# Casting one product's operand for the second pair earlier, and opening the first mixer's PSUM pools in the output stage

## The chip, the cores and the metric

The kernel runs on one NeuronCore of one Trainium2 chip. The metric is device time in microseconds (us); every kernel is run several times, and the median counts. All timelines are in microseconds from the start of the profiled span.

## The reference

The input is a sequence of 2048 rows of 1024 values. First comes a linear-attention block with 32 heads, then an MLP that mixes over the sequence (token mixer), each behind a layer norm and with a residual.

```python
def _A_ref(x, wqkv, wo):                       # linear attention, H = 32 heads of 32
    q, k, v = split_heads(x @ wqkv)
    phi = lambda t: where(t > 0, t + 1, exp(t)) + 1e-6
    pq, pk = phi(q), phi(k)
    kv, z = einsum("bhsd,bhse->bhde", pk, v), einsum("bhsd->bhd", pk)
    o = (pq @ kv) / (pq @ z + 1e-6)
    return merge_heads(o) @ wo

def _B_ref(x, w1, b1, w2, b2):                 # token mixer
    h = layernorm(x)
    u = gelu(einsum("bsd,sf->bdf", h, w1) + b1)     # 2048 -> 3584 over the sequence
    y = einsum("bdf,fs->bds", u, w2) + b2           # 3584 -> 2048
    return y.transpose(0, 2, 1)

h = x + _A_ref(layernorm(x), wqkv, wo)
out = h + _B_ref(layernorm(h), w1, b1, w2, b2)
```

## The kernel before

The program has four stages, one after the other on TensorE (PE): the projections for keys, values and queries; the output projection of the attention (the output stage), which also makes the residual `h`, its layer-norm statistics and the normalised rows `hE` (even row tiles) and `hO` (odd ones); the first mixer (w1 and gelu, giving `gE` and `gO`); and the second mixer (w2, written out). Around the change the order on each engine is the order in which the program is written, since nearly all instructions there are pinned (`Held`, `pin`).

**The mixer's scheme.** A mixer's matrix product is done as a two-by-two block product with seven products instead of eight (Strassen's scheme in Winograd's form). `Product7` holds the seven: `p1`, `p5`, `p6`, `p2`, `p7`, `p3`, `p4`. Each has a stationary operand `lhs[m]` made of weight blocks a11, a12, a21, a22, and a moving operand `mov[m]` made of `hE`, `hO` and the sums `hT2`, `hT3`, `hT4`. The results pass through PSUM tiles `psA`, `psB`, `psC`, `psE`: `p1` computes psA and ScalarE (ACT) copies it to psB; `p6` adds into psB and ACT copies that to psC; `p2`, `p7`, `p3` and `p4` add the rest, and each quarter ends in a gelu on ACT.

**Pairs and their pairs.** A `Quad` is a pair of `Mixer1` column blocks that share one set of weights (u = 0 to 6). Some of a pair's products are themselves done by seven smaller products (`Inner`: steps `i1`, `i6`, `i2`, `i5`, `i7`, `i3`, `i4`, with psI tiles of 256 columns). `interleave` puts the smaller products between pieces of the large ones, and calls functions at named points ("b", "c", "2", "7", "third", "end"). `run_first` does the pair u = 0, `run1` the pair u = 1, `run1_six` the rest.

**Product 7's operand.** It is a21 - a11, a tile named `sa` (tag `sa7`, one buffer). For u = 0 VectorE (DVE) makes it in the output stage. From u = 1 on `cast7(q)`, for the quarters q = 0 to 3, writes -a11 with an ACT instruction; after quarters 1 and 3 `add_a21` issues a DMA from POOL (line 164) that adds half of a21 from DRAM, 256 KB. `run1` calls the four at the points "c", "2", "7" and "third" of its first interleaved product. The matmuls of product 7 (`p7_fill`) use the eight blocks of the operand in the order 2, 3, 4, ... 7, 0, 1 (`first = NSP // 4`), so the third matmul already needs the second DMA. `cast5` does the same for product 5, with a22 as the cast half and the weight tile itself (`wq`) as the destination.

**The turn from the output stage to the first mixer.** The output stage works through 16 row tiles; it ends, for the last of them, with the ACT evacuations of two PSUM tiles `acc_t`, BN_STATS and BN_AGGR on DVE, `h_scale` (two small ACT instructions: Ln into `hln_l`, Exp into `sc_all`), `normalize_h` and the sums `sums_h` on DVE. Then the output stage's PSUM pools are closed, the mixer's pools `psz`, `psw`, `psx`, `psy` are opened, and `run_first` starts with `p1` of both column blocks, each with its copy from psA to psB behind it.

Helpers issue most of this, so nearly all of its instructions carry line 247, and the tile names tell them apart.

Of the kernel before, what the change touches and what calls it, by code (L numbers as in the profile page):

```python
# [16 lines left out]
PSUM = bass.MemoryType.PSUM  # L17
# [18 lines left out]
def kernel(  # L36
# [44 lines left out]
    def less_acc():  # L81
        accx.close()
        acc_ring[:] = [acc]
# [136 lines left out]
    hmov = {}  # L220
# [321 lines left out]
    class Quad:  # L542
# [251 lines left out]

        def run_first(self, nxt, before_inner, before_second):
            sts = self.sts
            for st in sts:
                st.p1()
            share(sts)
            for st in sts:  # L800
                st.p2()
            before_inner(slice(0, 2))
            self.in5.mov = self.mov5
            self.interleave(self.in5, self.steps(*[st.p6 for st in sts]), {
                "2": lambda: nxt.cast5(0), "7": lambda: nxt.cast5(1), "third": lambda: nxt.cast5(2), "end": lambda: nxt.cast5(3),
            })
            before_inner(slice(2, 4))
            nxt.begin1()
            self.base3()
            for i, st in enumerate(sts):  # L810
                st.apart = 1
                st.p7()
                before_second(slice(2 * i, 2 * i + 2))
            sts[0].p3()
            sts[1].p3_mm()
            self.late.append(sts[1].p3_evac)
            return sts, nxt
# [105 lines left out]
        def run1(self, pend, nxt, on_p4, third_sums, sums6):  # L923
            sts = self.sts
            s4, s6, s7 = self.steps(*[st.p4 for st in pend]), self.steps(*[st.p6 for st in sts]), self.steps(*[st.p7_fill for st in sts])
            c6, c7 = 3 * len(s6) // 4, len(s7) // 2

            def starting():
                self.in1.sums(slice(2, 4))
                self.in5 = Inner(sts, 5, self.mov5, next(Quad.tags), self.sink5, self.sum5)  # L930
                self.in5.sums(slice(0, 2))
                self.asums(6)
                self.t1 = self.base("t1a")
                for s, st in enumerate(sts):
                    st.begin(self.t1[:, s, :])

            def gelu(s, dh, t):
                return lambda: sts[s].evac(0, dh, t[:, s, :])

            def before_gelu():  # L940
                if third_sums is not None:
                    third_sums(slice(3, 4))
                gelu(0, 0, self.t1)()

            def gelu_late(*args):
                return lambda: self.late.insert(0, gelu(*args))

            self.in1.behind = self.late
            self.interleave(
                self.in1, s4, {  # L950
                    "b": starting, "c": lambda: self.cast7(0), "2": lambda: self.cast7(1),
                    "7": lambda: (self.in5.sums(slice(2, 4)), self.cast7(2)), "third": lambda: self.cast7(3),
                }, (("b", None), ("7", None))
            )
            in2 = Inner2(sts, 2, self.mov2, next(Quad.tags), self.add_to(self.t1), None)
            in2.sums()
            on_p4()
            nxt = nxt()
            share(sts)
            if third_sums is not None:  # L960
                third_sums(slice(0, 3))
            self.interleave(self.in5, s6[:c6], {
                "b": lambda: (sums6(slice(0, 1)), self.asums(3)), "third": lambda: (nxt.cast5(0), nxt.cast5(1)),
            }, flush=(("b", None), ("7", None), ("end", None)), first=1)
            sts[0].finish()
            self.base3()
            in3 = Inner2(sts, 3, self.mov3, next(Quad.tags), self.add_to(self.t3), None)
            in3.sums()
            sts[0].with_shared(sts[0].base3, sts[0].B)
            self.interleave(  # L970
                in2, s6[c6:] + s7[:c7], {
                    "2": lambda: (nxt.cast5(2), sums6(slice(1, 2))), "7": lambda: nxt.cast5(3), "third": lambda: (before_gelu(), sums6(slice(2, 4))), "end": gelu_late(1, 0, self.t1),
                }, (("7", None),)
            )
            sts[1].with_shared(sts[1].base3, sts[1].B)
            self.interleave(in3, s7[c7:], {
                "third": lambda: (gelu(0, 1, self.t3)(), nxt.begin1()), "end": gelu_late(1, 1, self.t3),
            }, (("b", 1), ("c", None)))
            return sts, nxt
# [13 lines left out]
    with ExitStack() as actx:  # L993
# [757 lines left out]
        with ExitStack() as a3:  # L1751
# [121 lines left out]
            def h_scale(i):  # L1873
                lnv = a3s.tile([P, 1], F32, name="hln_l")
                share_of = 1.0 / D if i in BY_ACT else 1.0
                hs.activation(lnv[:], mv_all[:, i, 1:2], ACT.Ln, bias=eps2[:], scale=(1.0 + LN_EPS) * share_of)
                hs.activation(sc_all[:, i:i + 1], lnv[:], ACT.Exp, scale=-0.5)
# [8 lines left out]
            def sums_h(us, which):  # L1886
                assert all(normal.issuperset(range(NSC * SPREAD.index(u), NSC * SPREAD.index(u) + NSC)) for u in us)
                ks = slice(NSC // 2 * us[0], NSC // 2 * (us[-1] + 1))
                e, o = hE[:, ks], hO[:, ks]
                for t in which:  # L1890
                    out, p, q = {
                        "t3": (hT3[:, ks], e[:, :, hi], o[:, :, hi]),
                        "t1": (e[:, :, hi], e[:, :, hi], e[:, :, lo]),
                        "t2": (hT2[:, ks], o[:, :, hi], e[:, :, hi]),
                        "t4": (hT4[:, ks], o[:, :, lo], hT2[:, ks]),
                    }[t]
                    hv.tensor_tensor(out, p, q, ALU.subtract)
# [52 lines left out]
            for i in range(1, NS):  # L1950
                if i > 1:
                    out_mm(i)
                if i in den_at:
                    den(den_at[i])
                if i in w1_at:
                    load_w1(*w1_at[i], pin, 4)
                if i >= SEEDED - 5:
                    load_xr(i + 5)
                if i == NS - 1:
                    h_scale(i - 1)  # L1960
                    normalize_h(i - 2)
                    normalize_h(i - 1)
                if 1 < i <= SEEDED:
                    h_mean(i - 1)
                if i - 3 in BY_ACT:
                    normalize_h(i - 3)
                if SEEDED - 2 <= i < NS - 2:
                    seed(i + 2)
                if i > 1:
                    out_evac(i)  # L1970
                if i - 3 in BY_DVE:
                    h_scale(i - 3)
                if i - 2 in BY_ACT:
                    h_var(i - 2)
                    h_scale(i - 2)
                if SEEDED < i < NS - 1:
                    h_scale(i - 1)
                if i in scale_at:
                    scale_q(*scale_at[i])
                for at in spread_at.get(i, ()):  # L1980
                    den_spread(*at)
                if i in sums_at:
                    cur = next(ahead)
                if i - 3 in BY_DVE:
                    normalize_h(i - 3)
                if i - 2 in BY_DVE:
                    h_var(i - 2)
                if SEEDED + 2 <= i < NS - 1:
                    normalize_h(i - 2)
                for at in sums_h_at.get(i, ()):  # L1990
                    sums_h(*at)
            h_scale(NS - 1)
            sums_h((1,), ("t1",))
            normalize_h(NS - 1)
            sums_h((0,), ("t1",))
            sums_h((0, 1), ("t2",))
            less_acc()

    earlyctx.close()
    actx_psum.close()  # L2000
    NT = 2
    psz = ctx.enter_context(tc.tile_pool(name="psz", bufs=NT, space=PSUM, reuse_waits="tile"))
    psw = ctx.enter_context(tc.tile_pool(name="psw", bufs=NT, space=PSUM, reuse_waits="tile"))
    psx = ctx.enter_context(tc.tile_pool(name="psx", bufs=NT, space=PSUM, reuse_waits="tile"))
    psy = ctx.enter_context(tc.tile_pool(name="psy", bufs=NT, space=PSUM, reuse_waits="tile"))
    gpool = ctx.enter_context(tc.tile_pool(name="gpool", bufs=1))
    gE = gpool.tile([P, NFP, D], FP16, name="gE")
    gO = gpool.tile([P, NFP, D], FP16, name="gO")
# [2 lines left out]
    assert NFP % 2 == 0 and NSP % 2 == 0 and NSP >= 4 and NFP >= 6  # L2011
    inner1 = mctx.enter_context(tc.tile_pool(name="inner1", bufs=1, side="right"))
    pools["i1"] = inner1
    hmov.update(moving(hE, hO, hT2, hT3, hT4))
    mov1, sums1 = inner_moving(hE[:, :, 0:CW], NSP, inner1, "hi1")
    mov5, sums5 = inner_moving(hE[:, :, CW:D], NSP, inner1, "hi5")
    mov2, sums2 = inner_moving(hO[:, :, 0:CW], NSP, inner1, "hi2")
# [13 lines left out]
    def quad1(u):  # L2031
        return Quad([Mixer1(2 * u), Mixer1(2 * u + 1)], mov1, mov5, mov2, mov3)

    Held.on = Held.scalar = True
    sums5()
    late = slice(0, NSP // 2)
    dve.tensor_tensor(hT3[:, late], hE[:, late, 0:CW], hT2[:, late], ALU.subtract)
# [198 lines left out]
```

## Time and profile before

| | |
|---|---|
| median of 3 runs | 551.63 us (550.24, 551.94, 551.63) |
| the profiled execution | 551.81 us |
| its span, first to last instruction | 550.0 us |
| mean granted TensorE clock | 0.997 |
| PE busy | 542.6 us, 99% of the span |
| DVE busy | 465.6 us, 85% |
| ACT busy | 312.5 us, 57% |
| POOL busy | 72.8 us, 13% |
| DMA | 77.76 MB, mean 141 GB/s |

A timeline row gives the start, the time from there to the end, the engine, the line, the operation, the tiles written and read, the shape and the count; in brackets stands how long the engine was idle just before and what ended that. Neighbouring instructions of one kind are merged into a row. "PEld" is PE's load of a stationary operand, which overlaps its matmuls. Instructions of one engine overlap a little in these rows, so the distance between two starts is what one really takes of the queue. The granted clock is a share of full speed.

### The profile page before, as it was taken

Reading aid. Unit: us, or ns where it says so; the run is one execution under the profiler, and the core shown is the slowest. Engines: PE = TensorE matmul, PEld = TensorE weight load, DVE = VectorE, ACT = ScalarE, POOL = GpSimd, SP = SyncE. Lnnn points to the kernel's source line nnn. Section 1 sums busy time; section 2 is a strip of 40 time slices with the busy share of each in tenths; the row PEclk is TensorE's granted clock in tenths of the full one; section 3 lists DMA queues with packets and bytes.
Section 4 is the critical chain, followed back from the end, with each engine's and each line's share of the span. In section 5 each row is a group of like instructions: output and inputs, shape, how many; then the busy total and the mean of one; then the engine's idle time right before and its main releaser. Section 6 shows DMA issues by size and latency. Waiting matters only on the chain.

```text
span 550.0 us, 10552 instructions
## 1 busy us (share of the span) xinstructions
PE 542.6 (99%) x4038; PEld 338.5 (62%) x4038; DVE 465.6 (85%) x926; ACT 312.5 (57%) x666; POOL 72.8 (13%) x78
## 2 busy tenths in 40 slices
PE   8999999999999999999899999999999999999997
PEld 3444446656864444456577777777455667877865
DVE  7798897867777578989689989999998899979877
ACT  5748677767787788657477677775320312412321
POOL 1000000000002440012012121130002103103111
PEclk9999999999999999999899999999999999999999
DMA  8933532201469999137345857656597659399344
GB/s 302 311 78 76 79 77 41 40 1 40 115 173 185 225 274 309 62 40 150 43 86 108 165 66 154 127 85 154 146 308 196 182 141 241 74 290 234 77 127 75
DMA packets 105378, 77.76 MB, mean 141 GB/s; under 512 B 16482, under 2 KB 97904, under 8 KB 105328
## 3 DMA queue, kind: packets, MB, share of 16 engines
q1 hardware_dynamic: 85536, 64.32, 42.0%
q0 software_dynamic: 19360, 12.34, 17.2%
q8 instruction: 31, 0.51, 0.4%
q10 hardware_dynamic: 432, 0.44, 0.2%
q14 instruction: 19, 0.16, 0.1%
HBM read 62.27 MB, written 11.67 MB: 134 GB/s over the span
## 4 chain that ended last, share of the span: by engine, by line
PE 84%; issue 5%; DMA 5%; DVE 3%; POOL 2%; ACT 1%; SPq 1%; POOLq 0%; ACTq 0%
PE psI L247 30%; PE psC L247 17%; PE psC L1195 4%; PE psB L1195 4%; PE psA L1195 4%; PE psB L247 4%; PE psA L247 3%; PE acc_t L1111 3%; PE acc_t L247 2%; PE psE L1195 2%; PE psA L1329 2%; PE psC L1329 2%; PE psB L1329 2%; DMA sa<-in_B_w_dram 2%; POOL h_bf L1843 2%
## 5 line engine op out<-in xcount | busy, mean ns | idle before, releaser
L247 PEld LDWEIGHTS <-is 128*128 128x128 f16 x900 | 88.5, 98 | 33.0 <-issue 0.8
L247 PEld LDWEIGHTS <-wq 128*128 128x128 bf16 (+1 forms) x694 | 67.9, 98 | 37.2 <-issue 0.7
L247 PEld LDWEIGHTS <-sa 128*128 128x128 f16 x467 | 45.7, 98 | 16.8 <-DMA sa<-in_B_w_dram 2.9
L247 PE MATMUL acc_t<-wo_sb,pqT 128*128 128x512 f16 x256 | 55.9, 379 | 0.0
L247 PEld LDWEIGHTS <-pqT 128*128 128x128 bf16 x256 | 24.8, 98 | 30.6 <-issue 1.1
L520 POOL DMA_DIRECT2D out_dram<-wq x28 | 24.3, 937 | 143.6 <-ACT wq L523 120.4
L247 PE MATMUL psC<-gs,wq 128*128 128x512 f16 x168 | 40.8, 379 | 0.0
L1843 POOL DMA_DIRECT2D h_bf<-in_A_x_dram x18 | 15.8, 984 | 185.6 <-DMA wq<-in_B_w_dram 169.7
L247 PE MATMUL psI<-hi,is 128*128 128x256 f16 x240 | 36.4, 275 | 0.0
L247 PE MATMUL psC<-hT,sa 128*128 128x512 f16 x112 | 32.9, 386 | 2.4 <-DMA sa<-in_B_w_dram 2.4
L247 PE MATMUL psC<-hT,wq 128*128 128x512 f16 x112 | 34.1, 379 | 0.0
L1195 PEld LDWEIGHTS <-xs 128*128 128x128 f16 x208 | 20.0, 98 | 22.2
L247 ACT COPY psI<-psI 128x256 f32<-128x256 f32 x60 | 21.5, 358 | 15.9 <-PE psI L247 13.8
L247 PE MATMUL psI<-gi,is 128*128 128x256 f16 x210 | 27.8, 273 | 0.0
L1195 PE MATMUL psA<-wkv,xnT 128*128 128x512 bf16 x104 | 26.7, 379 | 0.0
L164 POOL DMA_DIRECT2D wq<-in_B_w_dram x12 | 15.4, 1284 | 82.6 <-ACT wq L247 43.4
L1195 PEld LDWEIGHTS <-xnT 128*128 128x128 bf16 x156 | 15.3, 98 | 17.9 <-issue 0.2
L247 DVE TENSOR_TENSOR t<-psI,t 128x256 f32<-128x256 f32 (+1 forms) x45 | 20.2, 472 | 6.3 <-PE psI L247 5.0
L201 DVE TENSOR_SCALAR e_sb<-e_sb 128x512 bf16<-128x512 bf16 x64 | 18.1, 284 | 6.5 <-ACT e_sb L196 6.4
L164 POOL DMA_DIRECT2D sa<-in_B_w_dram x12 | 15.4, 1285 | 53.6 <-ACT sa L247 33.3
L1111 PE MATMUL acc_t<-wkv,xnT 128*128 128x512 bf16 x96 | 22.0, 379 | 0.1
L247 DVE TENSOR_TENSOR is<-wq 128x512 f16<-128x512 bf16 (+3 forms) x48 | 21.9, 457 | 0.0
(276 smaller groups left out, 1213.1 us busy)
## 6 DMA issues: line engine op xcount, KB each, us to landing
wq<-in_B_w_dram SPq DMA_DIRECT2D x20, 448.0 KB, 5.8
gs<-parked SPq DMA_DIRECT2D x9, 896.0 KB, 4.8
wq<-in_B_w_dram SPq DMA_DIRECT2D x11, 512.0 KB, 5.1
wq<-in_B_w_dram SPq DMA_DIRECT2D x5, 1024.0 KB, 7.2
shared_sb<-rd_dram SPq DMA_DIRECT2D x32, 128.0 KB, 5.1
out_dram<-h_bf SPq DMA_DIRECT2D x16, 256.0 KB, 5.1
x_sb<-in_A_x_dram SPq DMA_DIRECT2D x14, 256.0 KB, 3.9
w2o<-in_B_w_dram SPq DMA_DIRECT2D x4, 896.0 KB, 9.8
```

What stands on the lines that cost most here:

```text
L164: pin(nc.gpsimd.dma_start(t[:, ks, :], a21[:, ks, :], accum_op=ALU.add))
L201: pin(nc.vector.tensor_scalar(e_sb[:], e_sb[:], 1.0, PHI_EPS, ALU.min, ALU.add))
L247: return (lambda *a, **kw: pin(op(*a, **kw))) if self.always or getattr(Held, self.key) else op
L520: nc.gpsimd.dma_start(to, ot[:, a:b], accum_op=ALU.add)
L1111: mm = nc.tensor.matmul(pp[:, 0:CW], lhsT=xnT[:, kt, i * P:(i + 1) * P], rhs=wkv[:, kt, c * CW:(c + 1) * CW], start=(kt == 0), stop=(kt == ...
L1195: pin(nc.tensor.matmul(ps[:], lhsT=lhs[:, k, :], rhs=rhs[:, k, :], start=(start and k == 0), stop=(k == hk2 - 1), skip_group_check=True,))
L1329: pin(nc.tensor.matmul(out[:, j], lhsT=rhs[:, k, 2 * self.half + j, :], rhs=lhs[:, k], start=(start and j == 0 and k == 0), stop=(k == hk2 ...
L1843: pin(nc.gpsimd.dma_start(h_bfs[i][:, cols], x[rows(i), cols], accum_op=ALU.add))
```

## The change

Two things are done. First, `run_first` calls the four `cast7` of the next pair (u = 1) right after its two `p7`; `run1` leaves them out where the pair has the operand already. Second, the closing of the output stage's PSUM pools and the opening of the mixer's four pools move ahead of the last row tile's `h_scale`, and `p1` of the first column block (its matmuls and the copy from psA to psB) is issued there; `run_first` then issues only the second block's `p1`. On PE, DVE, POOL and SP the order of the instructions stays; on ACT the first psA copy now stands ahead of the last `hln_l` and `sc_all`, and the four casts stand behind the two `gO` gelus of product 7, ahead of the two `gE` gelus of product 3.

```diff
         def run_first(self, nxt, before_inner, before_second):
             sts = self.sts
-            for st in sts:
-                st.p1()
+            sts[1].p1()
             share(sts)
...
                 st.apart = 1
                 st.p7()
                 before_second(slice(2 * i, 2 * i + 2))
+            for q in range(4):
+                nxt.cast7(q)
             sts[0].p3()
             sts[1].p3_mm()
...
+            def cast(q):
+                return nop if 7 in self.S else partial(self.cast7, q)
+
             self.in1.behind = self.late
             self.interleave(
                 self.in1, s4, {
-                    "b": starting, "c": lambda: self.cast7(0), "2": lambda: self.cast7(1),
-                    "7": lambda: (self.in5.sums(slice(2, 4)), self.cast7(2)), "third": lambda: self.cast7(3),
+                    "b": starting, "c": cast(0), "2": cast(1), "7": lambda: (self.in5.sums(slice(2, 4)), cast(2)()), "third": cast(3),
                 }, (("b", None), ("7", None))
             )
...
+            less_acc()
+            a3p.close()
+            actx_psum.close()
+            NT = 2
+            psz = ctx.enter_context(tc.tile_pool(name="psz", bufs=NT, space=PSUM, reuse_waits="tile"))
+            psw = ctx.enter_context(tc.tile_pool(name="psw", bufs=NT, space=PSUM, reuse_waits="tile"))
+            psx = ctx.enter_context(tc.tile_pool(name="psx", bufs=NT, space=PSUM, reuse_waits="tile"))
+            psy = ctx.enter_context(tc.tile_pool(name="psy", bufs=NT, space=PSUM, reuse_waits="tile"))
+            Held.on = Held.scalar = True
+            hmov.update(moving(hE, hO, hT2, hT3, hT4))
+            cur.sts[0].p1()
             h_scale(NS - 1)
             sums_h((1,), ("t1",))
             normalize_h(NS - 1)
             sums_h((0,), ("t1",))
             sums_h((0, 1), ("t2",))
-            less_acc()
 
     earlyctx.close()
-    actx_psum.close()
-    NT = 2
-    psz = ctx.enter_context(tc.tile_pool(name="psz", ...))
-    psw, psx, psy likewise
...
-    hmov.update(moving(hE, hO, hT2, hT3, hT4))
...
-    Held.on = Held.scalar = True
     sums5()
```

More of the change, by code (lines that the diff above doesn't have):

```diff
@@ L1996 @@
             sums_h((0, 1), ("t2",))
-            less_acc()
     earlyctx.close()
-    actx_psum.close()
-    NT = 2
[L2002 to L2005, printed above, removed]
     gpool = ctx.enter_context(tc.tile_pool(name="gpool", bufs=1))
```

## The prediction

> **What bounds the kernel now.** I read the waits of TensorE (PE) first, since PE is busy nearly all the span: its table of waits has only three rows, each `us in total, times, longest`.
>
> ```profile
> PE psC L247 <- DMA sa<-in_B_w_dram: 2.4, 1, 2.4
> PE acc_t L104 <- DVE m L112: 1.2, 1, 1.2
> PE psA L247 <- ACT psB L247: 0.2, 1, 0.2
> ```
>
> The second is the program's start and is not touched. The first is one wait for product 7's operand (tile `sa`), the third one wait for the first copy psA to psB; these are exactly the two places of the change. So the time is PE's own work plus these gaps, and a change that leaves PE's work alone can win only there. The chain of waits shows what fed the first gap (start, duration, what):
>
> ```profile
> 250.49 1.28 POOL sa L164
> 251.77 1.79 issue
> 253.58 9.59 DMA sa<-in_B_w_dram
> ```
>
> The reader is to see that the second accumulating DMA was issued at 253.58 and landed only at 263.17. The timeline of PE at that place, and the windows view of the same stretch (length, busy time of PE, PEld, DVE, ACT, POOL, then the granted clock, DMA share and GB/s):
>
> ```profile
> 258.50 1.03 PE L247 MATMUL psB<-hT,sa 128*128 128x512 f16 x4
> 259.36 0.60 PE L247 MATMUL psI<-hi,is 128*128 128x256 f16 x4
> 259.80 0.60 PE L247 MATMUL psI<-hO,wq 128*128 128x256 f16 x4
> 260.24 0.59 PE L247 MATMUL psC<-hT,sa 128*128 128x512 f16 x2
> 263.21 0.61 PE L247 MATMUL psC<-hT,sa 128*128 128x512 f16 x1 [2.37 <-DMA sa<-in_B_w_dram]
> 263.61 1.06 PE L247 MATMUL psI<-hO,is 128*128 128x256 f16 x4
> 264.46 1.06 PE L247 MATMUL psI<-hi,is 128*128 128x256 f16 x4
> 265.31 1.06 PE L247 MATMUL psC<-hT,sa 128*128 128x512 f16 x2
> 266.17 0.79 PE L247 MATMUL psI<-hO,is 128*128 128x256 f16 x4
> 266.80 0.81 PE L247 MATMUL psC<-hT,sa 128*128 128x512 f16 x3
> ```
> ```profile
> 260.24:263.21 2.97, 0.60 (x5) 0.10 (x2) 1.25 (x3) 1.73 (x4) 0.94 (x1) 0.99 1.24 163
> 263.21:264.40 1.19, 1.19 (x5) 0.73 (x6) 0.00 (x0) 0.00 (x0) 0.34 (x1) 0.50 0.17 25
> 264.40:266.80 2.40, 2.40 (x13) 1.41 (x11) 1.12 (x2) 0.00 (x0) 0.00 (x0) 0.55 0.88 112
> 266.80:272.00 5.20, 5.20 (x40) 3.71 (x38) 4.86 (x10) 2.80 (x5) 0.00 (x0) 1.00 0.01 1
> ```
>
> The gap costs more than the 2.4 us that the table of waits says: after it the granted clock is 0.50, then 0.55, and back at 1.00 from 266.80.
>
> **The price of the gap.** At full clock four 512-wide matmuls take 259.36 - 258.50 = 0.86 us (0.215 each) and four 256-wide ones 259.80 - 259.36 = 0.44. From 260.24 to 266.80 PE issues five wide ones (2, 1, 2) and three groups of four narrow ones: 5 x 0.215 + 3 x 0.44 = 2.40 us of work in 6.56 us. So 4.16 us are lost: 2.54 of them idle (the third wide matmul was due at 260.24 + 2 x 0.215 = 260.67 and came at 263.21), and 1.62 at the lower clock.
>
> **Part one: the four casts of product 7 move ahead.** Nothing is added or removed: four ScalarE (ACT) instructions and two POOL DMAs for the second pair (u=1) are issued earlier, and the four later call points in `run1` become empty for this pair alone. PE, VectorE (DVE), SP and POOL keep their orders. Only ACT's changes: the casts now stand right behind the second `gO` and ahead of the `gE` of product 3. The rows of ACT there, before:
>
> ```profile
> 243.58 0.72 ACT L247 ACTIVATE gO<-t,b_sb 128x512 f16<-128x512 f32 x1 [1.20 <-DVE t L247]
> 245.56 0.72 ACT L247 ACTIVATE gE<-e,b_sb 128x512 f16<-128x512 f32 x1 [1.26 <-DVE e L247]
> 246.54 0.36 ACT L247 COPY psI<-psI 128x256 f32<-128x256 f32 x1 [0.26 <-PE psI L247]
> ```
> ```profile
> 248.33 0.63 ACT L247 ACTIVATE sa<-wq 128x512 f16<-128x512 bf16 x1
> 248.86 0.36 ACT L247 COPY t1a<-psI 128x256 f32<-128x256 f32 x1
> ```
> ```profile
> 249.57 0.62 ACT L247 ACTIVATE sa<-wq 128x512 f16<-128x512 bf16 x1
> ```
>
> A cast holds the queue 248.86 - 248.33 = 0.53 us, 0.10 less than its shown duration; I take 0.72 - 0.10 = 0.62 for a gelu. The casts wait for the old `sa` tile's last reader, product 7 of the first pair; the sum that the second `gO` reads was made from that product, so it is over by 243.58. Casts then start at 244.20, 244.73, 245.26 and 245.79, and leave ACT at 246.32. The second ends at 245.36. Before, its POOL DMA began 250.49 - (249.57 + 0.62) = 0.30 after it; so now at about 245.66, and the next at 246.94 (behind 1.28 of the first). How long such a DMA takes, from issue to landing, over all 24 of line L164:
>
> ```profile
> DMA to landing us min/median/max: 4.5/4.6/9.6
> ```
>
> At the median the second lands at 251.5, at the slowest at 256.5; PE wants it at 260.67. The cover is 4 us even at the worst price that the trace shows, so the gap goes whole, and with it the lower clock: **minus 4.16 us**. On POOL nothing stands between: the two DMAs for product 5 were issued ahead of these before, and still are.
>
> What is queued behind the casts on ACT: the `gE` of product 3 slips from 245.56 to 246.32 (what reads it, DVE's `finish`, belongs to the next pair), and the `psI` copy behind it from 246.54 to 246.94, ending at 247.30. Who waits for that copy is PE's sixth inner product:
>
> ```profile
> 247.42 0.60 PE L247 MATMUL psI<-hi,is 128*128 128x256 f16 x4
> ```
>
> It has 0.12 us left, so I cost the burst at nothing. If gelu and casts held ACT for their full shown durations, the copy would end at 243.58 + 0.72 + 4 x 0.63 + 0.72 + 0.36 = 247.90, and PE would be 0.48 late: that is the upper bound. A gain from ACT being freer at 248 to 253 is excluded, because PE has no other wait there.
>
> **Part two: the first copy psA to psB ahead of the last scale.** Before, ACT and PE ran:
>
> ```profile
> 227.97 0.29 ACT L247 ACTIVATE hln_l<-mv_all,eps 128x1 f32<-128x1 f32 x1 [1.28 <-DVE mv_all L247]
> 228.30 0.20 ACT L247 ACTIVATE sc_all<-hln_l 128x1 f32<-128x1 f32 x1
> 228.41 1.06 ACT L247 COPY psB<-psA 128x512 f32<-128x512 f32 x2
> ```
> ```profile
> 229.04 3.61 PE L247 MATMUL psA<-hO,wq 128*128 128x512 f16 x16 [0.19 <-ACT psB L247]
> ```
>
> PE stands 0.19 us until the first copy ends. Now the copy goes into the 1.28 us in which ACT waits for the last row's statistics. It can't start at once: with the pools opened here its PSUM bank is the one of the output stage's last tile, so it waits for the last of the BN_STATS:
>
> ```profile
> 226.41 1.29 DVE L247 BATCH_NORM_STATS2 hst<-acc_t 128x6 f32<-128x512 f32 x2
> 232.31 0.69 DVE L247 TENSOR_TENSOR hi<-hE 128x1024 f16<-128x1024 f16 x1
> ```
> ```profile
> 234.01 0.60 PE L247 MATMUL psI<-hi,is 128*128 128x256 f16 x4
> ```
>
> These end at 227.70; the copy runs from 227.72 and ends by 228.28 (1.06 / 2 and a tail), before PE is ready at 228.85: **minus 0.19 us**. In return the scale starts at about 228.25 instead of 227.97, and DVE's last normalisation, its subtractions and `hi` come up to 0.28 late: `hi` ends at 233.28 instead of 233.00, and PE, now at 233.82, still has half a microsecond. So the delay costs nothing and a loss is excluded; the part's other bound is no gain, 0.00.
>
> **The sum.** 4.16 + 0.19 = 4.35 us. The profiled execution took 551.81 us (550.0 of span), near the median of 551.63: 547.46 by the one, 547.28 by the other. I take 547.4.
>
> **What is late next.** After the gap the next thing that could hold PE is DVE, which was resting when the gap ended:
>
> ```profile
> 260.81 0.68 DVE L247 TENSOR_TENSOR hT<-hT 128x1024 f16<-128x1024 f16 x1
> 264.71 0.69 DVE L247 TENSOR_TENSOR t1a<-psI,t1a 128x512 f32<-128x512 f32 x1 [3.22 <-PE psI L247]
> ```
> ```profile
> 273.03 0.43 DVE L247 TENSOR_TENSOR is<-is,wq 128x512 f16<-128x512 f16 x1
> ```
> ```profile
> 274.13 0.60 PE L247 MATMUL psI<-hi,is 128*128 128x256 f16 x4
> ```
>
> Without the gap PE hands over the product of 264.71 at 260.24 + 3 x 0.215 + 0.44 + 0.25 = 261.58 (0.25 as before, 264.71 - 264.46), and DVE is free at 261.49: just in time. From there DVE follows PE as it did, and its operand `is` of 273.03 keeps 274.13 - 273.46 = 0.67 us of lead.
>
> **Rivals.**
> *The lower clock stays (0.09).* If the 0.50 to 0.55 has another cause than the gap, only 2.54 + 0.19 = 2.73 us go: 549.1. For it: the clock follows a mean over some time and the gap is short. Against it: the rows have 0.99 and 1.00 on both sides, and the drop begins at the gap's end. The Trainium skill ("TensorE: Matmul & The Clock Gate", section "What's actually happening") says that the clock falls to half after an idle window of about 3.4 us. By that rule a gap of 2.5 us would not bring it down, and this rival would hold; the trace here shows 0.50 behind a gap of 2.54 us and disagrees.
>
> *DVE becomes the bound (0.08), the slower side.* From 266.80 to 272.00 DVE is busy 4.86 of 5.20 us. Without its rest of 3.22 us it may fall behind by more than the 0.67 us of lead at 273.03; that is the point from which it decides. If PE then stops twice as long as it did once, with the clock's fall each time, 2 x 4.16 come back: 547.4 + 8.3 = 555.7. Against it: the rest was a wait for PE, no catching up.
>
> *The change doesn't reach the gap (0.06).* The table puts a wait to what came last; at 260 to 263 the weight loads ran too (DMA share 1.24). If PE waited for one of these, 0.19 goes: 551.5.
>
> *Part of it comes back (0.07).* ACT's burst (0.48) and a DVE lag of about half a microsecond together: 548.4.
>
> **How the numbers follow.** The forecast, 547.4, has 0.70. Range 546.5 to 549.5: below, 0.85 (half the spread of the three runs, 550.24 to 551.94); above, the rival of the clock and 0.4 of the burst's bound; the other two, 0.14, are left out. About 0.3%, 1.65 us, can be told from no change. Faster by more: 0.70 + 0.09 + 0.07 = 0.86; within: 0.06; slower: 0.08.
>
> **What would show it.** Right: no wait of PE for `sa`; POOL's first `sa` DMA near 245.7; clock 1.00 over the whole pair; `psA<-hO` with no wait for ACT; ACT's `psI` copy near 246.9. Wrong: a PE wait for `psI` near 247.4 (the burst), for `is` or `hi` behind 261 (DVE), or a clock under 0.9 with no gap ahead of it.

## The result and the profile after

| | before | after |
|---|---|---|
| median of 7 runs each | 550.24 us (548.69 to 551.94) | 547.36 us (547.11 to 547.90) |
| ratio | | 0.9944, 95% interval 0.9924 to 0.9963 |
| profiled execution | 551.81 us, span 550.0 | 547.90 us, span 546.1 |

The kernel is faster by 2.88 us between the medians and by 3.91 us between the two profiled executions. The forecast was 547.4. The waits of PE in the changed kernel, all that the view lists (in total, times, longest, us):

```profile
PE acc_t L104 <- DVE m L112: 1.2, 1, 1.2
PE psA L247 <- DVE hE L247: 0.3, 1, 0.3
PE psC L247 <- DMA gs<-parked: 0.2, 1, 0.2
PE tp L1428 <- DVE xn L1093: 0.2, 1, 0.2
```

The wait for `sa` is gone, and the wait of psA for ACT. PE's timeline where the gap had been, and the windows over it (the clock is the third number from the end):

```profile
260.13 0.81 PE L247 MATMUL psC<-hT,sa 128*128 128x512 f16 x3
260.77 0.60 PE L247 MATMUL psI<-hO,is 128*128 128x256 f16 x4
261.21 0.60 PE L247 MATMUL psI<-hi,is 128*128 128x256 f16 x4
261.65 0.59 PE L247 MATMUL psC<-hT,sa 128*128 128x512 f16 x2
```
```profile
256.00:262.00 6.00, 6.00 (x45) 4.21 (x43) 5.86 (x13) 4.54 (x10) 1.28 (x1) 1.00 0.92 182
262.00:268.00 6.00, 6.00 (x45) 4.21 (x43) 5.67 (x13) 2.79 (x5) 1.28 (x1) 1.00 0.40 50
```

All three wide matmuls follow each other, PE is busy all through both windows, and the clock stays at 1.00. The casts on ACT, POOL's DMAs and the PE step behind the copy:

```profile
244.10 2.17 ACT L247 ACTIVATE sa<-wq 128x512 f16<-128x512 bf16 x4
246.18 0.71 ACT L247 ACTIVATE gE<-e,b_sb 128x512 f16<-128x512 f32 x1
246.79 0.36 ACT L247 COPY psI<-psI 128x256 f32<-128x256 f32 x1
```
```profile
245.52 2.60 POOL L164 DMA_DIRECT2D sa<-in_B_w_dram  x2 [3.46 <-ACT sa L247]
```
```profile
247.31 0.60 PE L247 MATMUL psI<-hi,is 128*128 128x256 f16 x4
```

The copy begins at 246.79 and ends at 247.15; PE needs it at 247.31 and does not stop. The turn from the output stage, on ACT, DVE and PE:

```profile
228.16 0.57 ACT L247 COPY psB<-psA 128x512 f32<-128x512 f32 x1 [1.10 <-DVE hst L247]
228.65 0.30 ACT L247 ACTIVATE hln_l<-mv_all,eps 128x1 f32<-128x1 f32 x1
```
```profile
229.21 0.55 DVE L247 TENSOR_SCALAR hO<-h_bf,mv_all,sc_all 128x1024 f16<-128x1024 bf16 x1 [0.34 <-ACT sc_all L247]
232.98 0.69 DVE L247 TENSOR_TENSOR hi<-hE 128x1024 f16<-128x1024 f16 x1
```
```profile
228.86 3.62 PE L247 MATMUL psA<-hO,wq 128*128 128x512 f16 x16
233.83 0.60 PE L247 MATMUL psI<-hi,is 128*128 128x256 f16 x4
```

The first copy waits for BN_STATS, the scale comes late behind it and DVE stands 0.34 us for it. The operand `hi` that DVE makes is ready at 233.67, and PE takes it at 233.83.

### The profile page after: what moved, and what is told of

Read it like the earlier page. It is cut to its first block, busy times and chain, and to the rows that moved or that the text cites. A ratio compares the mean times of both kernels' runs of the same rounds, so it can differ in the third digit from the quotient of the medians.

```text
span 546.1 us, 10554 instructions
## 1 busy us (share of the span) xinstructions
PE 540.7 (99%) x4038; PEld 337.8 (62%) x4038; DVE 465.9 (85%) x926; ACT 312.7 (57%) x666; POOL 72.8 (13%) x78
## 4 chain that ended last, share of the span: by engine, by line
PE 88%; DMA 5%; DVE 3%; ACT 2%; issue 1%; POOL 0%; DVEq 0%; SPq 0%; POOLq 0%
PE psI L247 31%; PE psC L247 17%; PE psB L247 5%; PE psC L1198 4%; PE psB L1198 4%; PE psA L1198 4%; PE acc_t L1114 3%; PE psA L247 3%; DMA out_dram<-h_bf 2%; PE acc_t L247 2%; PE psE L1198 2%; PE psA L1332 2%; PE psC L1332 2%; PE psB L1332 2%; PE den_ps L247 1%
## 5 line engine op out<-in xcount | busy, mean ns | idle before, releaser
L164 POOL DMA_DIRECT2D wq<-in_B_w_dram x12 | 15.4, 1284 | 89.3 <-ACT wq L247 44.2
L1083 DVE BATCH_NORM_STATS2 st<-x_sb 128x6 f32<-128x512 bf16 x32 | 20.6, 681 | 0.9 <-DMA x_sb<-in_A_x_dram 0.9
```

What stands on the lines that cost most here:

```text
L164: pin(nc.gpsimd.dma_start(t[:, ks, :], a21[:, ks, :], accum_op=ALU.add))
L1083: return nc.vector.bn_stats(st[:, c, :], x_sb[:, c * CW:(c + 1) * CW])
```

## The experiments

The runs of before vary by over 3 us and those of after by under 1 us, and the gain of the medians (2.88) is less than what the first profile had lost at the gap (4.16). Two theories: the loss at the gap is not the same in each execution of before; or it is the same, and after gives about 1.3 us back elsewhere.

**Part one alone** (`e1_casts_only`): the kernel before with the four casts behind `p7`.

```diff
                 before_second(slice(2 * i, 2 * i + 2))
+            for q in range(4):
+                nxt.cast7(q)
...
-                    "b": starting, "c": lambda: self.cast7(0), "2": lambda: self.cast7(1),
-                    "7": lambda: (self.in5.sums(slice(2, 4)), self.cast7(2)), "third": lambda: self.cast7(3),
+                    "b": starting, "7": lambda: self.in5.sums(slice(2, 4)),
```

> Part one alone: the four casts of product 7 stand right behind the two p7 of the first pair, the PSUM pools and the first copy stay where they were. Theory of the varying gap (the gap ahead of product 7 is the whole gain, and it differs between executions of the kernel before, since the second adding DMA lands between 4.6 and 9.6 us after its issue): 547.5 us, nearly all of the change's gain, spread of the runs under 1 us, no wait of PE for sa, clock 1.00, the 0.2 us wait for the first copy still there. Rival (the gap costs 4.2 us in every execution of before, and after the change 1.3 us come back elsewhere, for instance through the burst of casts on ACT): also about 547.4, but with new PE waits of 1 us or more in the profile. Rival (the second part carries the gain): 550.

Measured: 547.39 us (547.05 to 548.19), ratio 0.9944 [0.9929, 0.9958]; no wait for `sa`, a wait of 0.3 for the first copy, the program's start 1.2 and one more of 0.2. The runs span 1.1 us, a little more than expected. Part one is the whole gain as far as the noise lets one tell, and PE has no new wait of 1 us anywhere.

**Part two alone** (`e2_copy_only`): the changed kernel with the casts where they were before.

```diff
-            for q in range(4):
-                nxt.cast7(q)
...
-                    "b": starting, "c": cast(0), "2": cast(1), "7": lambda: (self.in5.sums(slice(2, 4)), cast(2)()), "third": cast(3),
+                    "b": starting, "c": lambda: self.cast7(0), "2": lambda: self.cast7(1),
+                    "7": lambda: (self.in5.sums(slice(2, 4)), self.cast7(2)), "third": lambda: self.cast7(3),
```

> Part two alone: pools opened in the output stage and the first copy ahead of the last scale; the casts stay in the second pair. Theory of the varying gap: the time and the spread of the kernel before (548.7 to 552, ratio 0.998 to 1.002), a wait of PE for sa of 0.5 to 3 us in the profile, with a clock near half behind it if the wait is about 2 us or longer; the wait of PE for the first copy gone. Rival (the opening of the pools is itself worth over 1 us): ratio under 0.998.

Measured: 550.07 us (549.20 to 552.30), ratio 0.9990 [0.9976, 1.0004]. Nothing that can be told from zero. The gap was there, 2.0 us, with the clock at 1.00 behind it, where near half had been expected for a wait of that length; 3 of the 12 executions list a mean clock of 0.997.

**The whole change once more** (`a_again`).

> The changed kernel once more, beside the others: 547.4 us, spread under 1 us. It gives the distance of part one alone from the whole change (0.2 us by the prediction) and a second profile, in which both theories can look for waits: by the varying gap none over 0.3 us besides the program's start, by the rival 1 us or more in sum.

Measured: 547.80 us (547.02 to 548.14), ratio 0.9946 [0.9930, 0.9961]; PE waits 1.2 and 1.0 (for the first weights) at the program's start, and 0.2 for `is` behind 470. The runs span 1.1 us. Part one alone (0.9944) and the whole (0.9946) can't be told apart.

**The first copy without its wait** (`e5_other_bank`): the changed kernel with the line that opens `psy` put ahead of the one that opens `psx`.

> The changed kernel with the pools psx and psy opened in the other order, so that the first copy goes to a bank that the last output tile did not use and need not wait for the last BN_STATS. The copy should start as soon as product 1 of the first block is done, about 0.8 us ahead of the end of BN_STATS, and the last scale should no longer be late (0.54 us later than the aggregated statistics in the profile of after). Theory of the prediction (that delay is covered by the half microsecond that product 6 has to spare): the same time as the changed kernel within 0.2 us, 547.4. Rival (the delay of DVE reaches PE): 0.3 us faster, 547.0.

Measured: 547.46 us (546.85 to 548.44), ratio 0.9945 [0.9930, 0.9961]. ACT's rows:

```profile
228.47 0.57 ACT L247 COPY psB<-psA 128x512 f32<-128x512 f32 x1 [0.34 <-PE psA L247]
229.41 0.29 ACT L247 ACTIVATE hln_l<-mv_all,eps 128x1 f32<-128x1 f32 x1 [0.37 <-DVE mv_all L247]
```

The copy now waits for PE alone and the scale for DVE alone, as meant, though the copy started only 0.66 us ahead of the end of BN_STATS (229.13 here), and the time is the same, though 0.3 us could hide in the noise. The profiles say more: `hi` is ready 0.53 us ahead of PE here (234.43 and 234.96), 0.16 us ahead in the changed kernel (233.67 and 233.83). So the delay of the scale uses up part of that lead and does not reach PE.

**More profiles of the kernel before** (`b1`, `b2`, `b3`).

> The kernel before once more, one profile. Theory of the clock term (of the 4.2 us that the first profile lost at the gap, the 2.0 to 2.5 us of waiting are there in every execution, and the 1.6 us at half clock only in those that list a mean clock of 0.997): with a mean clock of 1.000 the profile has a gap of 2 to 2.5 us, a granted clock of 1.00 right behind it and a time of 549.5 to 551; with 0.997 it looks like the first and takes 551.5 or more. Rival (the gap itself varies from execution to execution): a gap under 1.5 us in a short execution.

> The kernel before, a further profile. By the theory of the clock term: a gap of 1.8 to 2.6 us; 549.5 to 551 with a granted clock of 1.00 behind it, 551.5 or more with about 0.5 behind it. Rival (the gap varies by more than 1 us): a gap under 1.5 or over 3 us.

> The kernel before, a further profile, with the same expectations as the one ahead of it: a gap of 1.8 to 2.6 us, and the time told by the clock behind it; by the rival a gap under 1.5 or over 3 us.

Measured: 549.49, 552.82 and 550.47 us, with mean clocks of 1.000, 0.997 and 1.000. PE at the gap, first in `b2`, then in `b3`, each with its window of 264 to 268:

```profile
261.18 0.59 PE L247 MATMUL psC<-hT,sa 128*128 128x512 f16 x2
264.16 0.47 PE L247 MATMUL psC<-hT,sa 128*128 128x512 f16 x1 [2.38 <-DMA sa<-in_B_w_dram]
264.42 1.06 PE L247 MATMUL psI<-hO,is 128*128 128x256 f16 x4
265.28 1.06 PE L247 MATMUL psI<-hi,is 128*128 128x256 f16 x4
```
```profile
264.00:268.00 4.00, 3.84 (x16) 2.35 (x17) 1.12 (x2) 0.00 (x0) 0.49 (x1) 0.57 0.62 78
```
```profile
260.00 0.60 PE L247 MATMUL psC<-hT,sa 128*128 128x512 f16 x2
263.49 0.39 PE L247 MATMUL psC<-hT,sa 128*128 128x512 f16 x1 [2.89 <-DMA sa<-in_B_w_dram]
263.71 0.60 PE L247 MATMUL psI<-hO,is 128*128 128x256 f16 x4
264.15 0.60 PE L247 MATMUL psI<-hi,is 128*128 128x256 f16 x4
```
```profile
264.00:268.00 4.00, 4.00 (x31) 2.82 (x30) 3.42 (x7) 1.08 (x2) 0.00 (x0) 1.00 0.56 71
```

Reckoned as in the prediction (from the third wide matmul's due time), the gap is 2.55 us in `b2` and 3.06 us in `b3`; in `b1` it is 1.89, in the first profile it was 2.54. The longest gap left the clock at 1.00: four narrow matmuls behind it take 0.44 us (263.71 to 264.15). A shorter one brought it down: 0.86 us (264.42 to 265.28). So the gap is there each time, 1.9 to 3.1 us, and the 1.6 us at half clock are not. The gap itself varies by 1.2 us, more than expected: 1.89 is under the 2 expected of `b1`, 3.06 is just over the rival's bound of 3. So both theories of a varying loss hold. All executions of before that ran beside the experiments, with these three, are 52: 13 list a mean clock of 0.997, with a median of 552.08, and 39 list 0.999 or 1.000, with 550.44. The distance is 1.64 us, close to the 1.62 us of the clock term. Of the 39 executions of kernels in which PE does not wait for `sa` (after, `a_again`, `e1`, `e3`, `e4`, `e5`) none lists less than 0.999.

What decides is where the gap falls. The lower clock stands for 3.41 us each time: from 263.14 to 266.55 in the first profile, from 264.35 to 267.76 in `b2`. In both the clock falls once more 286.72 us after it first fell, behind the last matmul of the program (549.86 and 551.07), and that is 84 times 3.413. So in these traces the clock changes only on a grid of 3.413 us, and the fall at the end (549.00 in `b3`) shows where the grid lies in an execution that has no other. The two windows of the grid at the gap, in the first profile, `b2` and `b3` (PE's busy time is the number behind the comma, the clock the third from the end):

```profile
259.72:263.14 3.42, 1.11 (x9) 0.56 (x6) 1.77 (x4) 1.92 (x4) 1.19 (x2) 1.00 1.27 176
263.14:266.55 3.41, 3.34 (x13) 1.94 (x14) 1.12 (x2) 0.00 (x0) 0.41 (x1) 0.50 0.68 88
```
```profile
260.93:264.35 3.42, 1.04 (x7) 0.43 (x6) 1.50 (x3) 1.92 (x4) 1.48 (x2) 1.00 1.20 165
264.35:267.76 3.41, 3.41 (x15) 2.11 (x14) 1.12 (x2) 0.00 (x0) 0.14 (x1) 0.50 0.69 86
```
```profile
258.86:262.28 3.42, 1.73 (x12) 0.98 (x10) 2.39 (x6) 1.92 (x4) 1.00 (x2) 1.00 1.33 209
262.28:265.69 3.41, 2.20 (x17) 1.60 (x18) 1.15 (x3) 0.00 (x0) 1.03 (x1) 1.00 0.82 103
```

Where one window held nearly the whole gap and PE was busy for only 1.04 or 1.11 us of it, the clock was halved for the window behind it. In `b3` an edge cuts the longer gap into 1.85 and 1.21 us, PE is busy 1.73 and 2.20 us, and the clock stays up. It stays up in the four other profiles with the gap too (`b1`, `e2`, `e6`, `e7`), where the emptiest window there has 1.85, 1.67, 2.31 and 1.93 us of busy time. So at this gap it is the idle share of one window that counts and not the length of the gap, with the bound between 1.11 and 1.67 us busy.

**Why the second add lands late: the weight loads** (`e4_half_load_behind`): the kernel before, with the larger of the two loads for u = 2 issued from POOL behind the second add. By the lists of DMA issues these loads have 512 and 1024 KB, and not 512 KB each, as the expectation below has it.

```diff
...
             if u < NQ1:
                 load_w1(u, 1)
-                load_w1(u, 0)
+                load_w1(u, 0, pin if u == 2 else (lambda ins: ins), q=nc.gpsimd if u == 2 else nc.sync)
```

> The kernel before, with one of the two 512 KB weight loads for the third pair issued from POOL behind the second adding DMA, instead of from SP at 252.2 beside it; the casts stay where they were. Theory that the second add lands late (9.6 us after its issue instead of 4.6) because the two weight loads take the DMA engines at the same time: it now shares them with one load and lands 1 to 3 us earlier; PE's gap shrinks from 2 to 2.5 us to under 1 us and the time is 548 to 549.3. Rival (the landing is late by itself, or because of the first add): the gap stays at 2 us or more and the time at 550 or above.

Measured: 547.55 us (547.52 to 547.99), ratio 0.9944 [0.9922, 0.9966], with the casts in their old place. PE's waits, and the landing times over the 24 DMAs of line L164:

```profile
PE acc_t L104 <- DVE m L112: 1.2, 1, 1.2
PE tp L1425 <- DVE xn L1090: 0.8, 1, 0.8
PE psA L247 <- ACT psB L247: 0.4, 1, 0.4
```
```profile
DMA to landing us min/median/max: 4.3/4.5/6.1
```

The slowest landing falls from 9.6 to 6.1 us, the second add's own is 5.4 us, and the gap is gone, more than expected. So it is the loads beside the add that make it late, the larger one above all. In the first profile the add did not even share the DMA engines with them at first: from 255 to 258.5, after its issue at 253.58, the view of the DMA queues lists packets of the loads' queue alone (packets, MB, share of 16 engines), and none of the queue of the adds:

```profile
q1 hardware_dynamic: 1996, 1.01, 104.8%
```

**The second add issued later** (`e6_casts_late`, then `e7_long_gap`). The kernel before, with casts 2 and 3 at "end" of in1; then at "7" of in5. The edit of `e7` is shown; in `e6` both casts stand under "end" in the first of the two places, and nothing else changes.

```diff
                 self.in1, s4, {
-                    "7": lambda: (self.in5.sums(slice(2, 4)), self.cast7(2)), "third": lambda: self.cast7(3),
+                    "7": lambda: self.in5.sums(slice(2, 4)),
...
             self.interleave(self.in5, s6[:c6], {
+                "7": lambda: (self.cast7(2), self.cast7(3)),
```

> The kernel before, with casts 2 and 3 moved later, from the points '7' and 'third' to 'end' of the same interleaved product, so that the second add is issued about 2 us later and the gap of PE gets longer. Theory that a gap of 2 to 2.5 us brings the clock to half only in some executions, by where it falls in a fixed window: a gap of about 4 us does it in nearly all, and each execution that lists a clock of 0.997 or less is 1.6 us longer than the rest; the time is 552.5 to 554.5. Rival (the clock follows the idle time alone, with one threshold): either all or none of the executions show it. If the landing is set by the weight loads, which end near 263, and not by the issue, the gap grows by less than the 2 us.

> The kernel before, with casts 2 and 3 moved into the next interleaved product (point '7' of in5, in the same pair), so that the second add is issued some 4 us later than in the kernel before, near 257.5. Moving them to 'end' had shifted the issue by 0.2 us only. Theory that a gap brings the clock down by where it falls in a fixed window (some executions at 2 us, all of them when it is long enough): the gap is 3.5 to 6 us, each execution lists a clock of 0.998 or less, the profile shows about 0.5 behind the gap, and the time is 553 to 556. Rival (the drop of the clock has nothing to do with the gap): executions with 1.000 are as frequent as in the kernel before, about 4 in 5, and the profile's clock is 1.00 behind the gap.

`e6` measured 551.45 us (549.60 to 552.96), ratio 1.0015 [1.0000, 1.0029], and says little: against PE's own progress (its `psA<-hO` row at 231.52) the second add was issued at 256.23, 24.71 us behind it, where `b1` has 253.48 - 228.94 = 24.54. The edit moved it by 0.2 us, and the gap, 1.96 us, did not grow. 6 of its 10 executions list 0.997; why more than of the kernel before is not shown. Its profile is one of them, but the clock fell at another place:

```profile
0.00:9.00 9.00, 6.36 (x26) 2.23 (x27) 5.16 (x24) 3.16 (x8) 1.90 (x8) 0.95 0.83 276
9.00:16.00 7.00, 7.00 (x40) 3.44 (x39) 4.87 (x13) 3.97 (x11) 0.00 (x0) 0.82 1.08 358
```

That is the program's start, where PE had waited 1.3 us in that execution. (The window of the grid ahead of that fall, 4.68 to 8.10, has 1.98 us of PE busy, so the bound found at the gap does not hold for the matmuls there; this stays open.) So a mean clock of 0.997 alone does not say that the drop was at the gap; in the two profiles of before that list it, the drop was there.

`e7` missed its expectation: 549.61 us (549.18 to 552.48), ratio 0.9990 [0.9973, 1.0007], with a gap of 1.98 us and the clock at 1.00 behind it; 1 of 10 executions lists 0.997. From its chain of waits, and PE:

```profile
258.41 4.57 DMA sa<-in_B_w_dram
```
```profile
263.03 0.39 PE L247 MATMUL psC<-hT,sa 128*128 128x512 f16 x1 [1.82 <-DMA sa<-in_B_w_dram]
```

Issued 4.9 us later than in `b1` (258.41 against 253.48), the add landed at 262.98 against 262.44. Here it took 4.57 us, like an undisturbed one: the loads were nearly through, and their queue moved only 0.07 MB from 259.5 to 263. So the later issue cost only half a microsecond because the earlier one had been held up by the loads. A longer gap was not reached, so these runs alone do not decide between the two theories, and whether a gap of 4 us or more always brings the clock down was not measured.

**The casts early, but in the second pair** (`e3_casts_at_c`).

```diff
-                    "b": starting, "c": lambda: self.cast7(0), "2": lambda: self.cast7(1),
-                    "7": lambda: (self.in5.sums(slice(2, 4)), self.cast7(2)), "third": lambda: self.cast7(3),
+                    "b": starting, "c": lambda: [self.cast7(q) for q in range(4)],
+                    "7": lambda: self.in5.sums(slice(2, 4)),
```

> The kernel before, with all four casts of product 7 at the point 'c' of the second pair's first interleaved product, where before only the first stood; nothing else changes. The second adding DMA should then be issued near 250.7 instead of 253.6. Theory that the gap is only a matter of when the second add is issued: it lands at 255.2 with the 4.6 us of an undisturbed one, at the latest at 260.3, so PE does not wait for it and the time is that of the whole change, 547.4 to 547.8. What it may cost: the copies to t1a and es behind the casts come up to 1.6 us later, and a PE wait of a few tenths may follow. Rival (it takes the place in the first pair, where ACT has idle time; in the second pair the burst of casts costs as much as it wins): 549 or more, with PE waits for psI behind ACT.

Measured: 549.12 us (547.93 to 549.74), ratio 0.9972 [0.9959, 0.9984]. There is no wait for `sa`, but PE waits here:

```profile
253.60 1.24 PE L247 MATMUL psB<-hT,sa 128*128 128x512 f16 x5 [0.43 <-ACT psB L247]
258.73 0.60 PE L247 MATMUL psI<-hi,wq 128*128 128x256 f16 x4 [0.19 <-DVE e L247]
```

The rival was half right: the early issue removes the gap, but the time is 1.3 to 1.8 us above that of the kernels with the casts in the first pair. The profile places 0.95 us of this in the second pair: from `psA<-hO` to the first `psC<-hT,sa` PE takes 32.15 us (229.18 to 261.33), in `e1` 31.20 (228.78 to 259.98). The rest is not located. The same burst in the first pair cost nothing: over the same stretch PE takes 31.27 us in after (228.86 to 260.13) and 31.20 in the first profile of before (229.04 to 260.24).

## Why the prediction was right, and where its sizes were off

- **Where PE's loss is.** Right: the only two waits that the change could reach were the two that went, and part one alone gives 547.39.
- **The idle part of the gap, 2.54 us.** Right as a typical size: 1.89, 2.55 and 3.06 us in three more profiles. The median of the four, 2.55, with the 0.2 to 0.4 us of the wait for the first copy, makes 2.75 to 2.95 us, close to the 2.88 between the medians.
- **The clock term, 1.62 us.** Mis-sized, and the main reason why the gain was 2.9 and not 4.35 us. It was read from one execution and taken as the price of each; only 13 of 52 list the mean clock that goes with it. The time forecast from the profiled execution, 547.46, held because that execution had paid the term and a kernel without the gap does not. That the median led to the same number was luck: the three runs known then had a median of 551.63, and from the 550.5 of the executions beside the experiments the same sum would give 546.2, under the stated range.
- **The rival of the clock and the rule beside it.** The rival (the lower clock has another cause) fell in the runs: no execution without the gap lists a mean clock under 0.999. The prediction took the fall of the clock to follow from the length of the gap; the runs showed that it follows from how much of one window of 3.413 us the gap fills. The Trainium skill ("TensorE: Matmul & The Clock Gate", section "What's actually happening") says that the window of about 3.4 us is free-running and does not start with the kernel. The traces here agree with that: by the grid, 3.06 us of idle left the clock up in `b3` and 2.55 us brought it down in `b2`. They do not agree with a whole idle window as the condition, since PE was busy for 1.04 and 1.11 us of the windows that brought it down.
- **The cover of the second add.** Right: issued at 245.52 and 246.8, expected 245.66 and 246.94. The slowest of these DMAs in after took 5.8 us. So the price "at the slowest 9.6 us" was not a property of the DMA; it was that of the two loads.
- **The burst on ACT.** Right: the copy at 246.79 (expected 246.94), PE not late. In the place of `e3` the burst was not free.
- **Part two, 0.19 us.** Not to be told from zero. The scale was late as worked out (DVE stood 0.34, expected up to 0.28). The half microsecond that `hi` was to have was 0.16 (233.67 to 233.83), since DVE was also later for another reason, which is not shown (its last BN_STATS began at 226.78, before at 226.41). It was enough.
- **DVE as the bound.** It did not come: no wait for `is` or `hi` behind 261 in after, and one of 0.2 us, behind 470, in `a_again`.

## What to carry to other kernels

Before pricing a gap from one profile, ask which part of it is there in each execution: the wait was, and its aftermath on the clock was not. The spread of the three runs (550.24 to 551.94) was a hint, and the mean clocks of further runs showed it. A DMA that feeds the next operand belongs ahead of the bulk loads that run beside it; putting one load behind it won as much as issuing it 7 us earlier. The burst of casts was free where ACT had idle time ahead of what others wait for, and was not free a few microseconds later.

## What the runs showed of the hardware that was not expected

A gap of PE of 2.5 us halved the granted clock for 3.41 us in two executions, and a longer one (3.06 us) left it alone: the clock changed only on a grid of 3.413 us that lies differently in each execution, and at the gap it fell where one window of the grid had PE busy for 1.04 or 1.11 us, not where the emptiest had 1.67 or more. An adding DMA of 256 KB landed 4.3 to 4.6 us after its issue when undisturbed (5.8 us behind another add issued 1.3 us ahead of it), and 9.0 to 10.1 us after it in the kernel before, beside loads of 512 and 1024 KB; for at least 3.5 us of this, none of its packets moved. Issued 4.9 us later, when the loads were nearly through, it landed 0.5 us later.
